# Forty idle products, an earlier key transpose and a reordered first four steps in a gated-recurrence attention plus PReLU network

## The chip, the cores and the metric

The kernel runs on one core of one Trainium2 chip. A core has TensorE (PE, matrix products, with weight loads listed apart as PEld), VectorE (DVE), ScalarE (ACT), GpSimd (POOL) and SyncE (SP, which here only issues DMAs). Each engine works through its own list of instructions in the order in which they stand, and waits on semaphores that other engines and DMAs raise. The metric is the device time of one execution in microseconds (us); lower is better.

## The reference

The first half is a recurrence with a gate, for 4 batches, 8 heads, 768 positions and head size 48. The second half is a two-layer network with a leaky activation over the 3072 tokens, from 384 to 2048 and back to 384. Everything is float32.

```
f = sigmoid(f_logit)
for t in range(768):
    state = f[:, :, t, :, None] * state + outer(k[:, :, t], v[:, :, t])     # 48 x 48 for each head
    y[:, :, t] = q[:, :, t] @ state
x = y.transpose(0, 2, 1, 3).reshape(3072, 384)
h = x @ w_in                                                # 384 -> 2048
g = maximum(h, 0) + alpha * minimum(h, 0)
out = g @ w_out                                             # 2048 -> 384
```

## The kernel before

The sequence is cut into 6 chunks of 128 positions, and the batches into 2 pairs; a *step* is one chunk of one pair, so there are 12 steps, numbered from 0. Steps 0 and 1 are the first chunk of either pair. The work of one step is written as four Python generators, and each `yield` ends a *piece*:

- `prepare` (letter P for the step itself, Q when it belongs to the next step): loads f, q, k and v by DMA, takes the sigmoid on ACT, and forms on DVE the products of gates that scale the queries and keys within a chunk. For chunks after the first, the scaled keys `ks` are turned by one DVE transpose into `kt` (line 424), and 16 small DMAs on SP's queue (line 429) put them in place as `ksn`. In the first chunk PE transposes them instead (`pk`, line 473).
- `carry` (O): PE forms the products across subchunks (`off`, lines 446 and 456) and the chunk's contribution to the state (`pd`, line 486).
- `attend` (S): PE forms the products within blocks of positions (`raw`, line 522, and `qu`, line 537), twice 64 rows each, once for each batch of the pair; DVE copies the wanted parts into `ad` (lines 528 and 543 or 559), ACT moves these into `A` (line 565), PE multiplies by the values and the state (`py`, line 576). ACT copies `py` to `y`, and `y` is put into the network's layout `xT`: by PE in step 0 (`xt`, line 594), by DMAs afterwards.
- `network` (n): 8 groups f0 to f7 of first-layer products (`ph`, line 619, 12 rows of the trace each), ACT's `neg` (line 624) and DVE's `gate` (line 626), DVE sums `S` after each four groups (line 700), then second-layer products (`po` in step 0, line 639; `pa` to `pe` with Strassen-like sums in the others, line 658). The network of one step runs within the attention of the next.

The weights arrive as 64-bit words and are converted in 8 pieces each: a and b are ACT's part of w_in and w_out (two passes over the upper halves, lines 201 and 203), w and v are DVE's part (`lead`, `rest`, `power`, `both`; lines 209, 222, 215, 227 or 229), where POOL issues the DMA that adds the leading part. A call of w forms the lead and power of one piece and finishes the piece before it. W forms sums of w_out's quarters (lines 712 to 720) in memory that the conversion has given back.

The order on PE, DVE and ACT is written out by hand: `first` holds a string of pieces for each of the first four steps, `usual` the one for all others, and the engines' instructions stand in the order in which the pieces are called. Orders on SP and POOL are the tile framework's. PSUM tiles come from two rings: `pair` (2 buffers of two banks, for the attention) and `bank` (4 buffers of one bank, for the network); a product that writes a buffer waits until the tile that had it before has been read.

A float32 product is two weight loads and two matmuls in PE's list, a transpose one of each, and a wait that doesn't fit into an instruction is one instruction more.

Of the kernel before, what the change touches and what calls it, by code (L numbers as in the profile page):

```python
# [8 lines left out]
F32 = mybir.dt.float32  # L9
# [15 lines left out]
NB = DB // 4  # L25
WP = 768
AT_ONCE = 1
RAWS, TOPS, POWERS, LEADS = 4, 3, 1, 4


@with_exitstack
def kernel(
# [30 lines left out]
    nc = tc.nc  # L63
    B, NC, _, HP, _ = qT.shape
# [7 lines left out]
    W = U * HP * C  # L72
# [25 lines left out]
    def bank(name):  # L98
        return psn.tile([128, 512], F32, tag="net", name=name)
# [16 lines left out]
    ones = const.tile([128, NS], F32, tag="ones", name="ones")  # L116
# [17 lines left out]
    for m in range(1, NB):  # L134
        lo = UO[m] + (4 if m == 1 else 0)
        n = NB - m
# [4 lines left out]
    for half in range(2):  # L141
        for m in range(1, NQ):
            n = NQ - m
# [23 lines left out]
    def load_weights(dst, src, name):  # L167
# [16 lines left out]
        words = src.rearrange("p (a n) -> p a n", a=rows_).bitcast(I16)  # L184
        at_once = AT_ONCE if rows_ > 1 else 0
        got = {}
# [66 lines left out]
    def quads(t):  # L253
        return t.rearrange("p (n r) -> p n r", r=4)

    def halves(cc):

        return slice(CH * cc, CH * cc + CH), slice(CH * (1 - cc), CH * (1 - cc) + D)

    def prepare(bp, c, x):  # L260

        i = f"{bp}_{c}"
# [3 lines left out]
        def load(name, src, bufs=2):  # L266
            t = work.tile([128, W], F32, tag=name, name=f"{name}_{i}", bufs=bufs)
            loads.dma_start(out=t.rearrange("p (u x) -> p u x", u=U),
                              in_=src[b0:b0 + U, c].rearrange("u p h t -> p u (h t)"))
            return t  # L270

        f = quads(load("f", fT, 1))
# [3 lines left out]
        for cc in range(NC2):  # L276
            t_, _ = halves(cc)
# [50 lines left out]
        def earlier(m):  # L328

            n = NB - m  # L330
            skip = UO[m - 1] + (8 if m == 2 else 4)
            nc.vector.tensor_tensor(  # L332
                us[:, :, UO[m]:UO[m] + 4 * n].rearrange("p g (i r) -> p g i r", r=4),
                us[:, :, skip:skip + 4 * n].rearrange("p g (i r) -> p g i r", r=4),
                fq[:, :, 1:1 + n].unsqueeze(3).broadcast_to((128, G, n, 4)), ALU.mult)
# [24 lines left out]
        ks = x["ks"] = work.tile([128, GC, 2, DB], F32, tag="ks", name=f"ks_{i}", bufs=1)  # L360
# [38 lines left out]
            earlier(6)  # L399
        nc.vector.tensor_tensor(ks[:, :, 0], kh, f32[:, 1:G:2].broadcast_to((128, GC, DB)), ALU.mult)  # L400
        if c:
            earlier(7)
        else:
            nc.vector.tensor_tensor(q16.rearrange("p g (i r) -> p g i r", r=4), q4[:, :, NQ:NB], g16[:, :, NQ:NB].unsqueeze(3).broadcast_to((128, G, NQ, 4)), ALU.mult)
# [14 lines left out]
                nc.scalar.copy(A[halves(cc)[1], :, par * HP:(par + 1) * HP, CH * cc:CH * (cc + 1)],  # L419
                               q3[rows(par)].rearrange("p (u h c) s t -> p u h c (s t)", h=HP, c=NC2)[:, :, :, cc, 0:CH])  # L420
        if c:

            kt = late["kt"].tile([128, W], F32, tag="kt", name=f"kt_{i}")
            nc.vector.transpose(kt, ks.rearrange("p g s t -> p (g s t)"))
            ksn = x["ksn"] = work.tile([128, U, HP * 128], F32, tag="ksn", name=f"ksn_{i}", bufs=1)
            for a in range(4):
                n = min(32, D - 32 * (a % 2))
                for b in range(NJ):
                    nc.sync.dma_start(
                        out=ksn[32 * b:32 * (b + 1)].rearrange("p u (h x) -> p (u h) x", h=HP)[:, :, 32 * a:32 * a + n],  # L430
                        in_=kt[32 * a:32 * (a + 1)].rearrange("p (g b x) -> p g b x", b=NJ, x=32)[:, :, b, 0:n])
# [257 lines left out]
    late = {}  # L689
# [12 lines left out]
    def halves_of_w_out():  # L702
# [12 lines left out]
        for to, x_, y_, op in ((t3, b22, b12, ALU.subtract), (t2, t3, b11, ALU.add), (t4, t2, b21, ALU.subtract),  # L715
# [3 lines left out]
                nc.vector.tensor_tensor(to[:, p], x_[:, p], y_[:, p], op)  # L719
            yield  # L720

    steps = [(bp, c) for c in range(NC) for bp in range(B // U)]
    first = (
        "P2 a P w P a P a w O P w S a w S Q a O a w S2 Q w S Q S",
        "P a w a P w2 b n2 v O n S b2 v n v n P S b S v n b n S v b v n Q b n b v O v Q n v W Q2 S2 W n Q n W Q W",
        "O W n2 S n2 S Q S n4 O S Q n Q2 n S2 n Q n Q n",
        "n2 S n S n Q n2 O Q O n2 S Q S n S Q n Q S Q n3",
    )
    usual = "S n2 S n2 O2 n Q n2 Q n2 Q S3 n Q S n Q n Q n"
# [6 lines left out]
    def begin(n):  # L736
        if n >= len(steps):
            return [None] * 4
        x = {}
        return [stage(*steps[n], x) for stage in (prepare, carry, attend, network)]  # L740

    with tc.manual_schedule(engines={mybir.EngineType.PE, mybir.EngineType.DVE, mybir.EngineType.Activation}):
        prep, car, att, net = begin(0)
        before = None
        for n in range(len(steps) + 1):
            coming, carried, following, after = begin(n + 1)
            on = pieces | {"P": prep, "O": car, "S": att, "n": before, "Q": coming}
            for key in (first[n] if n < len(first) else usual).split():
                for _ in range(int(key[1:] or 1)):
                    if on[key[0]] is not None:  # L750
                        next(on[key[0]])
            before, prep, car, att, net = net, coming, carried, following, after
# [55 lines left out]
```

## Time and profile before

| | |
|---|---|
| median of 4 runs | 636.97 us (635.4 to 639.11) |
| the profiled execution: its time / its span | 635.78 us / 634.0 us |
| mean granted TensorE clock | 0.994 |
| PE / PEld / DVE / ACT / POOL busy | 588.5 / 524.6 / 505.4 / 249.4 / 67.7 us |
| instructions on PE (matmuls, and as many loads) | 8108 |
| chain that ended last: PE / DVE / issue / ACT / DMA | 84 / 9 / 3 / 2 / 1 % |
| PE busy from 0 to 50 us / 50 to 100 us / 100 to 160 us | 15.7 / 46.0 / 57.9 us |
| PE busy from 300 to 500 us | 199.5 us of 200 |

The profile's times are microseconds from the first instruction's start. A line of a timeline has the start, the length, the engine, the source line, the operation and its tiles with the number of instructions merged, and in brackets the idle time before it with what ended it. "issue" as the cause of a wait means that the profile shows nothing that the engine waited for. PE's ends are modelled and its instructions overlap, so the length of a group is read from the start of one group to the start of the next. The granted clock is the share of full TensorE speed.

### The profile page before, as it was taken

How to read it: one execution, taken by the hardware profiler on the slowest of the kernel's cores; microseconds unless marked ns; L12 is line 12 of the kernel's file. 1: busy time of each engine (PE TensorE's matmuls, PEld its weight loads, DVE VectorE, ACT ScalarE, POOL GpSimd, SP SyncE). 2: the span in 40 equal slices, each digit the busy share in tenths (PEclk: the TensorE clock that was granted, in tenths of full speed). 3: DMA queues.
4: the chain of work that ended last, by engine and by line, in shares of the span. 5: the costliest groups of instructions: out<-in, count | busy, mean ns of one | idle time of the engine just before them, and what ended most of it. 6: DMA issues, size and time to landing. Idle time of an engine off the chain costs nothing.

```text
span 634.0 us, 18857 instructions
## 1 busy us (share of the span) xinstructions
PE 588.5 (93%) x8108; PEld 524.6 (83%) x8108; DVE 505.4 (80%) x1028; ACT 249.4 (39%) x466; POOL 67.7 (11%) x114
## 2 busy tenths in 40 slices
PE   0448799899999999999999999999999999999997
PEld 0447676789889889889889889889889889889997
DVE  5879969999799788888888888888888888762251
ACT  5667682531254053253253253253253253223110
POOL 9132222001001001001001001001001000000000
PEclk9999999989999999999999999999999999999999
DMA  7978987223223313223223222223223211201000
GB/s 243 298 208 217 284 254 163 50 70 78 50 77 85 63 58 84 64 56 84 56 64 84 46 75 85 52 68 84 47 73 79 55 38 26 38 17 26 26 1 25
DMA packets 73122, 56.30 MB, mean 89 GB/s; under 512 B 47408, under 2 KB 64944, under 8 KB 73040
## 3 DMA queue, kind: packets, MB, share of 16 engines
q0 software_dynamic: 10112, 27.53, 16.3%
q1 hardware_dynamic: 57536, 25.37, 15.8%
q10 hardware_dynamic: 5392, 2.21, 1.7%
q8 instruction: 64, 1.05, 0.7%
q14 instruction: 18, 0.15, 0.1%
HBM read 36.21 MB, written 4.72 MB: 65 GB/s over the span
## 4 chain that ended last, share of the span: by engine, by line
PE 84%; DVE 9%; issue 3%; ACT 2%; DMA 1%; DVEq 0%; SPq 0%; ACTq 0%
PE ph L619 38%; PE pc L658 9%; PE pa L658 9%; PE pe L658 5%; PE pd L658 5%; PE pb L658 5%; PE py L576 3%; PE raw L522 3%; PE qu L537 3%; PE pd L486 3%; DVE ad L528 1%; DVE ad L543 1%; PE off L446 1%; DVE t L719 1%; DVE gate L626 1%
## 5 line engine op out<-in xcount | busy, mean ns | idle before, releaser
L619 PE MATMUL ph<-xT,w_in_sb 128*128 128x256 f32 x1152 | 261.0, 385 | 4.0 <-issue 4.0
L619 PEld LDWEIGHTS ph<-xT,w_in_sb 128*128 128x128 f32 x1152 | 218.4, 192 | 36.9 <-issue 6.3
L624 ACT ACTIVATE neg<-ph 128x512 f32<-128x512 f32 x96 | 57.0, 596 | 199.8 <-PE ph L619 154.5
L626 DVE SCALAR_TENSOR_TENSOR gate<-neg,om,ph 128x256 f32<-128x256 f32 x192 | 82.1, 476 | 46.2 <-ACT neg L624 46.0
L658 PE MATMUL pa<-w_out_sb,gate 128*128 128x192 f32 x352 | 62.1, 329 | 0.0
L658 PE MATMUL pc<-t,S 128*128 128x192 f32 x352 | 61.7, 329 | 0.0
L658 PEld LDWEIGHTS pa<-w_out_sb,gate 128*128 128x128 f32 x352 | 57.8, 190 | 1.9 <-DVE gate L626 1.3
L658 PEld LDWEIGHTS pc<-t,S 128*128 128x128 f32 x352 | 57.3, 190 | 0.6
L528 DVE COPY_PREDICATED ad<-mraw,raw 128x256 f32<-128x256 int32 (+1 forms) x96 | 42.3, 440 | 7.6 <-PE raw L522 5.1
L543 DVE COPY_PREDICATED ad<-mquad,qu 128x224 f32<-128x224 int32 (+6 forms) x140 | 42.0, 300 | 6.2
L565 ACT COPY A<-ad 32x256 f32<-32x256 f32 x96 | 38.5, 401 | 1.4
L419 ACT COPY A<-q 48x512 f32<-48x512 f32 x44 | 27.1, 617 | 30.1 <-DVE q L370 29.7
L332 DVE TENSOR_TENSOR us<-us,fs 128x768 f32<-128x768 f32 (+5 forms) x60 | 37.0, 617 | 0.0
L289 DVE TENSOR_TENSOR qd<-qd,f 128x768 f32<-128x768 f32 (+2 forms) x36 | 27.2, 755 | 6.3 <-ACT qd L284 6.3
L576 PEld LDWEIGHTS py<-A,vs 128*64 128x64 f32 x768 | 25.5, 145 | 7.2 <-ACT A L565 4.3
L576 PE MATMUL py<-A,vs 128*64 128x64 f32 x768 | 27.5, 232 | 3.9 <-ACT A L565 3.9
L676 ACT COPY o<-pa 128x192 f32<-128x192 f32 x11 | 3.5, 317 | 69.7 <-PE pa L658 58.5
L700 DVE TENSOR_TENSOR S<-gate 128x512 f32<-128x512 f32 x44 | 30.3, 688 | 0.8
L658 PE MATMUL pe<-w_out_sb,S 128*128 128x192 f32 x176 | 30.5, 327 | 0.4 <-ACT o L676 0.4
L658 PE MATMUL pb<-t,gate 128*128 128x192 f32 x176 | 30.4, 326 | 0.0
L658 PE MATMUL pd<-w_out_sb,S 128*128 128x192 f32 x176 | 30.4, 326 | 0.0
L522 PEld LDWEIGHTS raw<-qd,k 48*32 48x32 f32 x1536 | 18.5, 109 | 14.1 <-issue 13.1
(109 smaller groups left out, 742.0 us busy)
## 6 DMA issues: line engine op xcount, KB each, us to landing
w_out_raw<-in_w_out SPq DMA_DIRECT2D x8, 767.8 KB, 6.5
w_in_raw<-in_w_in SPq DMA_DIRECT2D x8, 767.2 KB, 6.9
f<-in_fT POOLq DMA_DIRECT2D x11, 512.0 KB, 4.5
q<-in_qT POOLq DMA_DIRECT2D x11, 512.0 KB, 4.1
k<-in_kT POOLq DMA_DIRECT2D x11, 512.0 KB, 5.0
out<-o SPq DMA_DIRECT2D x24, 192.0 KB, 2.1
vs<-in_v POOLq DMA_DIRECT2D x22, 192.0 KB, 4.8
w_out_sb<-w_out_lead POOLq DMA_DIRECT2D x8, 384.0 KB, 5.5
```

Source lines behind the costliest of these rows:

```text
L289: nc.vector.tensor_tensor(qdv[d], qdv[d - 1][:, :, :, 1:5 - d], f[:, :, 1:5 - d].rearrange("p (g i) r -> p g i r", i=NB), ALU.mult)
L332: nc.vector.tensor_tensor(us[:, :, UO[m]:UO[m] + 4 * n].rearrange("p g (i r) -> p g i r", r=4), us[:, :, skip:skip + 4 * n].rearrange("p g ...
L522: nc.tensor.matmul(raw[DB * j:DB * (j + 1), par, hp * C:hp * C + QW], lhsT=k[r_, g * DB:(g + 1) * DB], rhs=qd[r_, g], start=True, stop=True)
L528: nc.vector.copy_predicated(adu[:, :, :, d:4], mraw[:, d, :, d:4].bitcast(I32).unsqueeze(1).broadcast_to((128, H, NB, n)), rv[:, :, QO[d]: ...
L543: nc.vector.copy_predicated(ad[:, u, :, :, 4 * m:DB], mquad[:, lo:lo + n].bitcast(I32).unsqueeze(1).unsqueeze(1).broadcast_to((128, 2, HP, ...
L565: nc.scalar.copy(A[s_, u, :, s_], ad[s_, u].rearrange("p r h t -> p (r h) t"))
L576: nc.tensor.matmul(py[64 * par:64 * par + 64, u, o:o + CH], lhsT=vs[bp][:, cc, u, hd * D:hd * D + 64], rhs=A[:, u, par * HP + hp, CH * cc: ...
L619: nc.tensor.matmul(ph[:, j * T:(j + 1) * T], lhsT=w_in_sb[:, kt, m * 128:(m + 1) * 128], rhs=xT[:, kt], start=(kt == 0 and j == 0), stop=( ...
L624: nc.scalar.activation(neg, phv, AF.Relu, scale=-1.0)
L626: nc.vector.scalar_tensor_tensor(gate[:, m % NH, m // NH], neg[:, j], om[:, m:m + 1], phv[:, j], ALU.mult, ALU.add)
L658: nc.tensor.matmul(to[:, 0:DH], lhsT=of(f), rhs=by(f), start=(f == 0 and not more), stop=(f == NH - 1), skip_group_check=True)
L700: nc.vector.tensor_tensor(to, x_, y_, op)
```

## The change

Forty products of 32 x 8 over the constant tile `ones` are put at the head of PE's list; nothing reads their bank. The transpose `kt` moves from the last piece of `prepare` into the piece before it, directly behind the `ks` that it reads; its DMAs stay in the last piece. The four strings of `first` are replaced. `usual` stays.

```diff
+IDLE = 40
 ...
         nc.vector.tensor_tensor(ks[:, :, 0], kh, f32[:, 1:G:2].broadcast_to((128, GC, DB)), ALU.mult)
         if c:
+            kt = x["kt"] = late["kt"].tile([128, W], F32, tag="kt", name=f"kt_{i}")
+            nc.vector.transpose(kt, ks.rearrange("p g s t -> p (g s t)"))
             earlier(7)
 ...
         if c:
-
-            kt = late["kt"].tile([128, W], F32, tag="kt", name=f"kt_{i}")
-            nc.vector.transpose(kt, ks.rearrange("p g s t -> p (g s t)"))
+            kt = x["kt"]
             ksn = x["ksn"] = work.tile([128, U, HP * 128], F32, tag="ksn", name=f"ksn_{i}", bufs=1)
 ...
+    idle = bank("idle")
+
     first = (
-        "P2 a P w P a P a w O P w S a w S Q a O a w S2 Q w S Q S",
-        "P a w a P w2 b n2 v O n S b2 v n v n P S b S v n b n S v b v n Q b n b v O v Q n v W Q2 S2 W n Q n W Q W",
-        "O W n2 S n2 S Q S n4 O S Q n Q2 n S2 n Q n Q n",
+        "P2 a w P2 a P a w O P w S a w S Q a O S a w S Q S Q w S",
+        "P a w a P w2 b n2 O v n b S b v n v n P n S b S v b n S v b v n Q b n O b v Q n v2 W Q2 S2 n Q W n Q W Q W",
+        "O W n2 S n3 S2 n Q n2 O S Q n Q2 n S2 n2 Q n Q",
         "n2 S n S n Q n2 O Q O n2 S Q S n S Q n Q S Q n3",
     )
 ...
     with tc.manual_schedule(engines={mybir.EngineType.PE, mybir.EngineType.DVE, mybir.EngineType.Activation}):
+        for _ in range(IDLE):
+            nc.tensor.matmul(idle[0:32, 0:8], lhsT=ones[:, 0:32], rhs=ones[:, 0:8], start=True, stop=True)
         prep, car, att, net = begin(0)
```

In the lists of the engines this comes to the following. PE: 160 instructions more at the head (two loads and two matmuls for each product); in step 1 the network's group f5 moves ahead of the second `raw` (12 rows), and in step 2 the group f4. DVE: in step 0 the first lead and power stand ahead of line 323; the w that stood before step 1's line 323 stands behind line 355; in step 1 gate f5 moves ahead of the second line 528, the two scans (lines 319 and 321) ahead of a piece of w_out, and the first sums of w_out (line 719) behind line 414; in step 2 gates f4 and f5 move forward with their groups; in all steps from the third on the transpose stands 7 to 12 instructions sooner. ACT: step 0's sixth pass over w_in goes between the two halves of line 565, and some `neg` and conversion passes change places in steps 1 and 2. SP: the first ksn DMAs go ahead of a store of `out`. POOL: two of the loads of v and one of f go ahead of one DMA of the conversion.

## The prediction

> **What bounds the kernel now.** I read the page's slices first, then the windows, the chain of waits, and the PE, DVE and ACT timelines up to 165 us.
>
> From the page (busy tenths in 40 slices; the DMA queue of PE's instructions):
>
> ```profile
> PE   0448799899999999999999999999999999999997
> DVE  5879969999799788888888888888888888762251
> ...
> q8 instruction: 64, 1.05, 0.7%
> ```
>
> From the windows (length, PE busy and instructions, PEld, DVE, ACT, POOL, clock, DMA):
>
> ```profile
> 300.00:400.00 100.00, 99.79 (x1342) 90.91 (x1341) 86.95 (x182) 36.89 (x73) 6.76 (x10) 1.00 0.26 65
> ```
>
> After about 165 us PE has no gap worth naming, so its work there is fixed. The end can move only by time that PE loses before that. From PE's timeline:
>
> ```profile
> 18.49 1.08 PE L446 MATMUL off<-q,kh 48*32 48x32 f32 x64 [18.49 <-DVE q L370]
> 20.12 1.44 PE L456 MATMUL off<-us 48*32 48x16 f32 x128 [0.55 <-DVE us L404]
> 21.49 1.97 PE L473 MATMUL pk<-ident,ks 128*128 128x128 f32 x8
> 23.39 0.75 PE L522 MATMUL raw<-qd,k 48*32 48x80 f32 x22
> 26.76 0.96 PE L522 MATMUL raw<-qd,k 48*32 48x80 f32 x38 [2.62 <-issue]
> ...
> 33.01 0.91 PE L522 MATMUL raw<-qd,k 48*32 48x80 f32 x38 [2.31 <-issue]
> ...
> 39.00 1.20 PE L486 MATMUL pd<-vs,ksn 64*48 64x48 f32 x44 [2.17 <-issue]
> ...
> 76.95 9.48 PE L619 MATMUL ph<-xT,w_in_sb 128*128 128x256 f32 x36 [3.97 <-issue]
> ...
> 126.17 1.07 PE L537 MATMUL qu<-us,k 48*32 48x112 f32 x64 [1.52 <-DVE ad L543]
> ```
>
> Four stops have no releaser. Between the first two lie 42+64+21 = 127 matmuls, between the next two 43+64+20 = 127, with as many loads and two waits: 256 instructions. q8 carries 64 packets of 1.05 MB / 64 = 16 KB, which is 256 of PE's instructions each, and the trace has its packets at 23.7, 30.8, 36.6 and 74.6 us, one near each stop. So PE runs out of instructions. The block after next is asked for when PE enters a block, and in this stage (DMA share 0.8 to 1.0) arrives 5.5 to 6.6 us later: 20.1 to 26.76, 26.76 to 33.01, 33.01 to 39.00, 71.48 to 76.95. A block of small products lasts 2 to 4 us. Later blocks last longer, and packets start about 1 us behind the boundary: no stops.
>
> From ACT's timeline, and from DVE's:
>
> ```profile
> 11.99 0.99 ACT L203 ACTIVATE w_in_neg<-w_in_raw,bias 128x768 int16<-128x768 uint16 x1
> ```
>
> ```profile
> 11.70 1.26 DVE L323 TENSOR_TENSOR us<-us,f 128x1024 f32<-128x1024 f32 x1
> ...
> 14.75 0.55 DVE L209 TENSOR_TENSOR w_in_lead<-w_in_pos,w_in_neg 128x768 bf16<-128x768 bf16 x1
> ...
> 48.41 1.23 DVE L323 TENSOR_TENSOR us<-us,f 128x1024 f32<-128x1024 f32 x1 [2.98 <-ACT us L316]
> ```
>
> Up to 18.5 us DVE sets the pace. From 40.2 us it is ACT: vs, a pass over w_in, eight A copies, four us copies, and y at 48.52. From 88 to 162 us DVE runs without a break; PE waits for it at 123 and 125 us.
>
> **The change, part by part.**
>
> *Lead and power ahead of line 323 (step 0).* They need ACT's neg, which ends at 11.99+0.99 = 12.98; DVE is free at 11.79. Line 323 starts at 12.98+0.05+0.86 (the pair's 14.84 to 15.70) = 13.9 instead of 11.8; the 0.86 no longer stands before line 376. Net +1.25: the first off at 19.75, the second (line 456) at 21.4.
>
> *The idle products.* They wait only for POOL's `ones` (2.1 us) and end long before 18 us even at 0.12 us a row, so their 80 rows cost nothing; the cover is DVE's first chain, and without it they would cost up to 10 us. They shift every block boundary by 160 instructions = 80 rows. The stops then fall on row 79 of line 456, rows 6 and 5 of the two qu, and row 4 of py. The block for the first is asked for 31 instructions behind the first off, which carries only a wait of its own. Does PE's sequencer run that far past a waiting product? One row says yes: the packet of 53.04 us belongs to a boundary on the eighth load of ph, executed at 55.5 us, and lies behind a product whose input (xT, ACT) ended at 52.19; 0.85 us would be the shortest lag of the busy stage, where 1.9 to 4.0 is usual. I take yes: the first block is there by about 12 us. Then, with about 6 us per block: line 456 ends 22.8, pk 24.7, raw 26.4; block asked for at 21.9, there at 28.0; qu to 29.1, raw to 30.75, five rows of qu; next block 34.0; qu to 35.1, pd 35.1 to 37.0 (1.92 for its two parts) instead of 40.20. The next block, at 40.0, is no later than ACT's A copies. **-3.2 at y** (45.3). Bounds: all three stops gone, 1.25-7.1 = -5.9; the sequencer held, first block at 26.0, pd to 41.1: +0.85.
>
> A rule speaks against this. The Trainium skill, "Runtime: NRT & Kernel Launch", section "Instruction fetch mechanics", says that crossing a 16 KiB boundary is mostly hidden; by it the shift is worth nothing and this part +1.25. The four stops of 2.2 to 4.0 us decide for the trace.
>
> *Clock.* pk's 8 transposes take 472 ns each at 21.5 us and 272 at 61.9: PE is slow through the first attention, though the profile lists 1.00. It is listed at 0.50 from 76.5 to 79.9, 3.5 us into the stop. The idle products end some 10 us before the first off, so I give them no gain in speed (bounds: 0, and the 0.9 + 0.3 + 1.0 us by which pk, off and pd exceed their later rows).
>
> The skill's "TensorE: Matmul & The Clock Gate", Part 1, has full speed lost after one idle window of about 3.4 us; by it the gain is zero too.
>
> *Step 1.* The w moved behind line 355 leaves DVE's idle 2.98 and stands in its busy part: 1.76. Line 404 ends at 45.3+11.24+1.73 = 58.3 where PE has done off at 56.6: PE waits 1.6. The block boundary now lies on row 94 of line 456, asked for as off starts (55.8), there at 61 to 62.4: 2.4 more. The next one is on row 8 of qu: 0 to 1.6, take 0.8. With f5 ahead of the second raw, the boundary there has 36 ph rows (8.07) as cover, and the stop of 3.97 goes; with it the half clock (36 rows in 9.33 instead of 8.07: 1.26), of which I put 0.95 back at 56 to 62 us. Sum +0.5, bounds -2 and +2.5. PE reaches po 2.7 earlier. DVE: -3.2+1.76; its idle 2.64+1.72+0.81 at 79 to 88 goes; new idle before line 528, f5 and f7 of 3.8 and 0.7 of slow clock: **-2.1**.
>
> *Step 2.* f4 (2.7 us) ahead of the second raw covers PE's 0.26+1.52, and the half clock of 127.7 to 131.1 (28 rows in 7.93 instead of 6.2) goes: PE 6.2 earlier at line 658's pc. But pc reads S, whose last sum ended at 143.84 where pc began at 145.57, in DVE's unbroken stretch. DVE moves by -2.1, so pc by -2.1-1.73 = **-3.8**. The moved sums of w_out and scans are the same DVE work in another order: 0.
>
> *Transpose sooner, SP's and POOL's order.* In the later steps kt (1.16) passes lines 680 to 682. These free the bank of f0: ready at 305.34, used at 306.94; still 0.44 to spare. ksn's DMAs come about 2.5 us sooner; pd's first products are 0.23 apart in every step, whatever the DMAs do, so that gains only the 0.07 gaps. The store between ksn DMAs waits up to 1 us, and 12 DMAs behind it; they still end 2 us sooner than before. Loads of v and f ahead of one conversion DMA (2 us of POOL's queue): that piece lands about 60 us, used after 66. Shifted boundaries in later steps: one block, near 170 us, of 2.5 us. Together 0, bounds -0.5 and +1.5.
>
> Sum: 635.78-3.8 = 632.0 for an execution like the profiled one, which lies 1.2 under the median; against 636.97 it is **633.2**.
>
> **Rivals.** (1) The sequencer is held by off's wait. For: the other blocks were all asked for as PE reached them. Against: the packet of 53.04. Then +0.85 at y, and DVE's gain is used up: 637.6, slower if blocks take 6.6 rather than 6 us each.
> (2) More stops go: blocks asked for earlier meet a quieter DMA system (5 us each): -5.9 at y and less in step 1: 629.5 to 630.
> (3) Slower: the transpose eats the bank's slack. From 0.44 us of further delay on, f0 waits in each of 8 steps; at 1.16-0.44+0.3 = 1 us each, +8-3.8: 641. Against: DVE's own work before line 680 is unchanged.
>
> **How the numbers follow.** Main case 0.58 (own range 630.5 to 636), rival 1 0.20, rival 2 0.14, rival 3 0.08. About 0.5% (3.2 us) tells a change from none: faster is under 633.8. Main gives 0.36 faster and 0.22 same; rival 1 0.02, 0.13 and 0.05 slower; rival 2 0.14 faster; rival 3 0.08 slower. Range 629.5 to 638.5.
>
> **What would show it.** Right: the first off at 19.7; no stop in line 456 of step 0, stops in both qu near 26 to 28 and 31 to 34; y near 45.3; a stop of 3 to 5 us in line 456 of step 1; none behind the second qu there; clock 1.00 at 127 us; pc following S at once near 141; PE 99.8% busy after. Wrong: a first stop in line 456 of step 0 (rival 1), ph waiting for line 681 in late steps (rival 3).

## The result: no difference that can be measured, and the profile after

The changed kernel takes 637.61 us (median of 45 executions, 632.85 to 642.56), the kernel before 638.37 us (71 executions, 632.05 to 640.75). The ratio is 0.9991, with a 95% interval of 0.9978 to 1.0004: 0.6 us less, between 1.4 us less and 0.3 us more. Forecast were 3.8 us less.

The four times that the prediction had of the kernel before were low: their median of 636.97 is 1.4 us under that of 71 executions, and the execution that was profiled, 635.78, is 2.6 us under it. The profiled execution of the changed kernel, 633.21 us (span 631.4), is 4.4 us under its own median. So the two profiles, set side by side, show a gain of 2.6 us; the medians of all executions differ by 0.8. Single executions of either kernel lie further apart than the whole forecast.

From the changed kernel's page: the slices of PE, DVE and the granted clock, and the queue of PE's instructions.

```profile
span 631.4 us, 19021 instructions
...
PE   2458989999999999999999999999999999999997
...
DVE  5889899999799698888888888888888888762251
...
PEclk9958999999999999999999999999999999999999
...
q8 instruction: 65, 1.06, 0.7%
```

From its windows (length, PE busy and instructions, PEld, DVE, ACT, POOL, clock, DMA share, GB/s):

```profile
0.00:50.00 50.00, 22.58 (x671) 19.53 (x672) 36.67 (x70) 31.64 (x52) 23.36 (x56) 0.83 0.85 250
...
300.00:400.00 100.00, 99.82 (x1456) 90.51 (x1455) 86.83 (x183) 38.20 (x74) 6.76 (x10) 1.00 0.28 66
```

The late steps look as before, PE without a gap. 65 packets of instructions instead of 64: 160 instructions more. From PE's timeline:

```profile
2.16 4.44 PE L747 MATMUL idle<-ones 128*32 128x8 f32 x80 [2.16 <-POOL ones L119]
19.66 1.08 PE L447 MATMUL off<-q,kh 48*32 48x32 f32 x64 [13.07 <-DVE q L371]
21.30 0.98 PE L457 MATMUL off<-us 48*32 48x16 f32 x79 [0.55 <-DVE us L407]
25.28 0.71 PE L457 MATMUL off<-us 48*32 48x16 f32 x49 [3.01 <-issue]
25.92 1.97 PE L474 MATMUL pk<-ident,ks 128*128 128x128 f32 x8
...
30.01 0.77 PE L538 MATMUL qu<-us,k 48*32 48x52 f32 x58 [0.57 <-issue]
...
34.59 1.01 PE L538 MATMUL qu<-us,k 48*32 48x52 f32 x59 [1.84 <-issue]
35.94 1.53 PE L487 MATMUL pd<-vs,ksn 64*48 64x48 f32 x64 [0.34 <-PE qu L538]
...
47.07 4.26 PE L595 MATMUL xt<-y,dense 128*128 128x256 f32 x12 [1.70 <-ACT y L586]
...
58.93 1.25 PE L457 MATMUL off<-us 48*32 48x16 f32 x128 [1.74 <-DVE us L407]
...
76.24 5.45 PE L620 MATMUL ph<-xT,w_in_sb 128*128 128x256 f32 x24
...
137.24 0.59 PE L659 MATMUL pa<-w_out_sb,gate 128*128 128x192 f32 x2 [1.24 <-DVE gate L627]
...
141.05 2.76 PE L659 MATMUL pc<-t,S 128*128 128x192 f32 x16
```

The 80 idle rows are over at 6.6 us. The first off is at 19.66. Then come stops without a releaser, each at the start of an instruction block: row 79 of the second off, row 6 of the first qu, row 5 of the second. The packet of instructions for the first of these stops starts at 22.8 us, and the profile has none of PE's queue, q8, ahead of that. From the DMA view of the changed kernel, 22.8 to 23 us:

```profile
q8 instruction: 1, 0.02, 39.6%
```

xt is at 47.07 where it was at 49.73. The stop of 3.97 us behind step 1's second qu is gone, and pc begins at 141.05 where it began at 145.57.

**How to read a gain in this kernel.** DVE's timelines give one line for each kernel that carries the rest: the last idle time ahead of its unbroken stretch. Of the changed kernel:

```profile
84.89 0.56 DVE L210 TENSOR_TENSOR w_out_lead<-w_out_pos,w_out_neg 128x768 bf16<-128x768 bf16 x1 [0.81 <-ACT w_out_neg L204]
```

Of the kernel before:

```profile
87.98 0.56 DVE L209 TENSOR_TENSOR w_out_lead<-w_out_pos,w_out_neg 128x768 bf16<-128x768 bf16 x1 [0.81 <-ACT w_out_neg L203]
```

From there to the last product there are 543.1 and 542.6 us. Over all 18 profiles of kernels with the full work (these two and 16 below) it is 541.9 to 544.3 us, but for two in which DVE waits once more at 94 us. And from the end of step 0's pd to xt it is 9.5 to 9.6 us in all of them, whatever the order of pieces. So an execution is: the end of pd in step 0, plus 9.6, plus xt to DVE's arrival at that line, plus about 543. Only the first and the third of these terms vary by much: 35.3 to 41.4 and 36.1 to 42.8 us.

### The profile page after: what moved, and what is told of

It reads as the page before. It is cut to its first block, busy times and chain, and to the rows that moved or that the text cites. A ratio compares the mean times of both kernels' runs of the same rounds, so it can differ in the third digit from the quotient of the medians.

```text
span 631.4 us, 19021 instructions
## 1 busy us (share of the span) xinstructions
PE 593.2 (94%) x8188; PEld 528.1 (84%) x8188; DVE 506.6 (80%) x1028; ACT 249.4 (39%) x466; POOL 66.6 (11%) x114
## 4 chain that ended last, share of the span: by engine, by line
PE 71%; DVE 17%; issue 6%; DMA 2%; POOL 2%; ACT 1%; ACTq 0%; DVEq 0%; POOLq 0%
PE ph L620 31%; PE pc L659 8%; PE pa L659 8%; PE pe L659 5%; PE pd L659 4%; PE pb L659 4%; PE py L577 3%; PE qu L538 2%; PE raw L523 2%; PE pd L487 2%; DVE gate L627 2%; DVE ad L529 2%; DVE qd L290 2%; DVE ad L544 1%; DVE S L701 1%
## 5 line engine op out<-in xcount | busy, mean ns | idle before, releaser
L538 PE MATMUL qu<-us,k 48*32 48x112 f32 (+1 forms) x1536 | 26.7, 256 | 3.5 <-issue 2.4
```

The costliest lines, as they stand in the source:

```text
L538: nc.tensor.matmul(qu[DB * j:DB * (j + 1), par, hp * QS + 4:hp * QS + QL], lhsT=k4[r_, g * DB:(g + 1) * DB], rhs=us[r_, g, 4:QL], start=Tr ...
```

## The experiments

All times are set against the kernel before on the same chip (11 to 35 executions of it); 0.1% is 0.64 us. Differences of means, where given, carry their standard error.

### The three parts, alone and together

The change has three parts: idle products (I), the sooner transpose (T), the four strings (S). Their edits:

```diff
I  +        for _ in range(IDLE):
   +            nc.tensor.matmul(idle[0:32, 0:8], lhsT=ones[:, 0:32], rhs=ones[:, 0:8], start=True, stop=True)
T  +            kt = x["kt"] = late["kt"].tile([128, W], F32, tag="kt", name=f"kt_{i}")
   +            nc.vector.transpose(kt, ks.rearrange("p g s t -> p (g s t)"))
                earlier(7)
S  -        "P2 a P w P a P a w O P w S a w S Q a O a w S2 Q w S Q S",
   +        "P2 a w P2 a P a w O P w S a w S Q a O S a w S Q S Q w S",   (and the other three)
```

I alone: 

> The kernel before with the 80 idle products and nothing else. Two readings of the missing gain. The fetch reading: PE's first block after the first off is asked for only when that off runs, and then comes 4.6 to 6.6 us later, execution by execution; the two profiles at hand are two draws of it. By it the first off stays at 18.5, a stop of 3 to 5 us falls on row 79 of the second off, two shorter ones into the two qu; y is 2 to 4 us earlier than before if a fetch takes 4.6 to 5.4 us as in the profile after, 1 us earlier if it takes 6; the stop of 3.97 us at 73 us is gone; the ratio is 0.994 to 0.998. The reading that the idle products gain nothing in the middle execution: ratio 0.999 to 1.001, and whatever is gained by 165 us is lost later, because the blocks are shifted in the later steps too (the profile after lost 1.3 us between 159 us and the end).

S and T, without I: 

> The changed kernel without the idle products. The fetch reading: the first off at 19.7, the old four stops of 2 to 3 us about 1.2 later than before, y 1.2 us later; step 1 loses no stop at 73 us if f5 stands ahead of the second raw; step 2 gains 1.8 us in ad; sum 0 to +1.5 us, ratio 1.000 to 1.002. The reading in which the strings are worth nothing or cost more: ratio 1.003 or above, and then the idle products are a gain that the strings take away.

T alone: 

> The kernel before with the keys transposed sooner and nothing else. My prediction gave it 0 in the later steps. If it is the cause of the 1.3 us that the profile after lost between 159 us and its end: +1 to +1.5 us, ratio 1.002, with small PE gaps at L446 to L537 of the later steps. If it costs nothing: ratio 0.999 to 1.001, and the profile keeps its distance from the profile before from 165 us on within 0.3 us.

All three again: 

> The changed kernel once more, for a second profile and for times beside the parts on the same chip. The fetch reading: again the first off at 19.7 and the first stop on row 79 of the second off, but with fetches that last anything from 4.6 to 6.6 us, so that y lies between 45 and 49; ratio 0.998 to 1.000. The reading that all executions gain 2.6 us, and the equal medians are chance: ratio 0.995 to 0.997.

I and S: 

> The changed kernel with the transpose at its old place: idle products and strings only. On the chip so far, against before: idle products alone 0.9946, strings with transpose 0.9964, transpose alone 1.0016, all three 0.9991 and 0.9994. The reading of a common cap: idle products and strings take away the same waits of DVE ahead of its unbroken stretch (88 to 162 us before), so together they bring no more than the larger of them, and the transpose takes 1 to 2 us back in the later steps: ratio 0.994 to 0.9965. The reading of a clash: the two harm each other in step 1 or 2 whatever the transpose does: ratio 0.998 to 1.000.

S alone: 

> The kernel before with the four new strings alone. Common cap: strings with transpose (0.9964) less the transpose's 1.0016: 0.993 to 0.996. Clash: the same, since there is nothing to clash with. If the ratio is 0.996 to 0.998, the transpose cost nothing beside the strings.

I and T: 

> The kernel before with idle products and the sooner transpose, old strings. Common cap: the two act in different places and add up: 0.9946 times 1.0016 = 0.996, between 0.994 and 0.998. Clash of idle products and transpose (the shifted instruction blocks meet the moved transpose in the later steps): 0.999 or above, the value of the whole change.

| parts | ratio to before | 95% interval | difference of means, us |
|---|---|---|---|
| I | 0.9946 | 0.9918 to 0.9975 | -3.1 (0.9) |
| T | 1.0016 | 0.9996 to 1.0037 | +1.5 (0.5) |
| S | 0.9929; again 0.9962 | 0.9900 to 0.9957; 0.9935 to 0.9988 | -4.2 (0.8); -2.1 (0.9) |
| I T | 0.9965 | 0.9940 to 0.9990 | -1.9 (0.8) |
| S T | 0.9964 | 0.9939 to 0.9990 | -2.0 (0.7) |
| I S | 0.9975 | 0.9949 to 1.0000 | -1.4 (0.7) |
| I S T | 0.9991; again 0.9994 | 0.9978 to 1.0004; 0.9972 to 1.0016 | -0.5 (0.4); -0.3 (0.6) |

Two things follow. The transpose costs where it is added: 1.5 us alone, 1.2 beside I, 0.9 beside I and S, and beside S 2.2 or 0.1, by which run of S is taken; hardly one of them is certain by itself. And I and S each bring 2 to 4 us alone, but 1.4 together, between what the common cap and the clash had expected. The ratios of I alone and T alone lie where the fetch reading and the loss in the later steps had them; S with T is better than either reading allowed.

### Where the transpose costs

Only steps 2 and 3 take the transpose sooner (there `c == 1`), the others as before:

```diff
-        if c:
+        if c == 1:
             kt = x["kt"] = late["kt"].tile([128, W], F32, tag="kt", name=f"kt_{i}")
             nc.vector.transpose(kt, ks.rearrange("p g s t -> p (g s t)"))
```

> The changed kernel with the transpose sooner only in steps 2 and 3, and at its old place in steps 4 to 11. If the loss of the transpose lies in the later steps (0.1 us in each, at the products of f0 behind qu, which wait for line 681): the profile keeps its distance to before from 165 us on, and the time is 0.7 to 1 us under that of the changed kernel, ratio 0.997 to 0.9985. If it lies in steps 2 and 3: as the changed kernel, 0.999 to 1.000.

Measured: 0.9955 (0.9933 to 0.9977), 2.0 us under the changed kernel; more than expected, and in the direction of the late steps. I and S with the transpose at its old place everywhere have 0.9975 on the same chip, so none of the cost is left. From DVE's arrival to the last product it is 542.8 us here, and 543.6 on average (542.7 to 544.3) in the six profiles with the whole T, against 542.7 (541.9 to 543.1) in the nine without T; the two profiles in which DVE waits once more are left aside. The transpose alone shows the place. DVE of that kernel in a late step:

```profile
400.20 1.25 DVE L403 STREAM_TRANSPOSE kt<-ks 128x1024 f32<-128x1024 f32 x1
...
403.99 0.35 DVE L681 TENSOR_TENSOR o<-Csum,pb 128x192 f32<-128x192 f32 x1
```

Its PE, at the end of step 2 and in the same late step:

```profile
162.66 5.45 PE L619 MATMUL ph<-xT,w_in_sb 128*128 128x256 f32 x24 [1.54 <-DVE Csum L680]
...
403.73 1.16 PE L537 MATMUL qu<-us,k 48*32 48x112 f32 x62
404.81 0.48 PE L619 MATMUL ph<-xT,w_in_sb 128*128 128x256 f32 x1
```

DVE of the kernel before in that late step:

```profile
400.39 0.35 DVE L681 TENSOR_TENSOR o<-Csum,pb 128x192 f32<-128x192 f32 x1
```

And its PE:

```profile
401.37 1.04 PE L537 MATMUL qu<-us,k 48*32 48x112 f32 x62
402.37 2.83 PE L619 MATMUL ph<-xT,w_in_sb 128*128 128x256 f32 x12
```

Lines 680 to 682 read the banks that the next network groups write. Before, line 681 ended at 400.74 and f0 began at 402.37, 1.63 us later. With the transpose ahead of it, it ends at 404.34 and f0 begins at 404.81, still 0.47 later, but 1.08 behind qu's start instead of 1.00. Between 175 and 600 us the stretches from qu to the network's next group grow by 0.6 to 0.7 us in sum in the four profiles of T, S T and I S T (two); without T they grow by 0.3 us at most. The rows show no idle time of PE there, so that f0 is late because of its bank is argued, not shown. Where f0 comes early it is shown: at 162.66 it waits 1.54 us for line 680. I T has this wait too (1.60 us); the kernels with the new strings don't, so for them the late stretches are what is left.

### The phase of PE's instruction blocks

One block is 256 of PE's instructions, which are 64 idle products. n of them move every later boundary by 2n rows. The first four kernels are the new strings with the old transpose, and differ only in this number:

```diff
-IDLE = 40
+IDLE = 0 / 64 / 4 / 56
```

0: 

> The kernel before with the new strings alone, once more, as the base of three kernels that differ from it only in the number of idle products. Expected 0.993 of before, 0.991 to 0.996. Its instruction blocks end on row 22 of the first raw, row 21 of the second and row 20 of pd in step 0, and in step 1 on row 26 of the first raw and row 51 of the second qu: profile with a stop of 2 to 3 us there, near 75 to 80 us.

64: 

> New strings and 64 idle products, which are 256 instructions: exactly one block more, so every boundary in the attention lies on the row where it lies without idle products. The reading that idle products act only by shifting the blocks: as the strings alone, within 0.2%, profile with the stop on row 51 of step 1's second qu. The reading that the products themselves do the harm (or the good), by the array, its clock, or the bank that they take: as with 40 of them, 0.9975.

4: 

> New strings and 4 idle products, 8 rows of shift. The block reading, with a fetch of about 5.5 us: in step 0 boundaries on rows 14, 13 and 12 of raw, raw and pd, as good as without; in step 1 on row 18 of raw (5.9 us behind the boundary before it), row 17 of the ph group behind the first qu (5.0 us) and row 43 of the second qu (5.4 us): every block has nearly its fetch time, and the stop of 2 to 3 us at the second qu goes; 2 to 2.5 us less than the strings alone, ratio 0.989 to 0.991. If the phase is nothing: as the strings alone.

56: 

> New strings and 56 idle products, a phase that should be bad: in step 1 a boundary on row 62 of the second off comes 3.2 us behind the one before, and one on row 3 of the ph group behind the second qu 2.1 us behind the one before it: stops of 2.3 and 3.4 us by a fetch of 5.5 us, where the strings alone have one of 2.5. Step 0 as without idle products (rows 38, 37 and 36). Block reading: 2.5 to 3.5 us more than the strings alone, ratio 0.997 to 0.999. If the phase is nothing: as the strings alone.

56 again, on another chip: 

> New strings, transpose at its old place, 56 idle products, once more, to see whether 0.9908 (6 executions) stands. If the phase of the instruction blocks is what counts: 0.989 to 0.993. If it was the draw: 0.995 to 0.997, as the strings alone and with 64.

The whole changed kernel with 56: 

> The changed kernel with 56 idle products in place of 40, and nothing else. If the change is lost to the phase at 40 and to the transpose: 0.992 to 0.995, the phase of 56 less 0.2% for the transpose. If the phase is nothing: 0.998 to 1.000, as the changed kernel.

The kernel before with 56: 

> The kernel before with 56 idle products and nothing else: old strings, old transpose. If the phase of the blocks is what 56 brings, the strings being worth little beside it: 0.989 to 0.994. If 56 is good only with the new strings, whose group f5 stands between its two boundaries of step 1: as with 40 idle products alone, 0.994 to 0.997.

The changed kernel with 40 at the head and 16 more ahead of xt in step 0, so that the blocks of 40 hold in step 0 and those of 56 from step 1 on:

```diff
         if not (bp or c):
+            more = bank("more")
+            for _ in range(16):
+                nc.tensor.matmul(more[0:32, 0:8], lhsT=ones[:, 0:32], rhs=ones[:, 0:8], start=True, stop=True)
```

> The changed kernel with its 40 idle products at the head and 16 more directly ahead of xt in step 0, where PE waits 1.7 us for y: step 0 keeps the blocks of 40, and from step 1 on they lie as with 56. Between 0.9992 (40) and 0.9908 (56) lie 5.4 us. By the profiles (4 with 40 and the new strings, 3 with 56) 2.0 us of it lie ahead of pd's end in step 0 and about 1 us in step 1, at row 94 of the second off. If step 0 makes most of it: 0.996 to 0.999. If step 1 and later make most of it: 0.991 to 0.994.

| strings, transpose | idle products | ratio to before | 95% interval |
|---|---|---|---|
| new, old | 0 | 0.9962 | 0.9935 to 0.9988 |
| new, old | 64 | 0.9967 | 0.9945 to 0.9988 |
| new, old | 4 | 0.9923 | 0.9896 to 0.9951 |
| new, old | 56 | 0.9908; again 0.9903 | 0.9878 to 0.9938; 0.9869 to 0.9938 |
| new, sooner | 40 | 0.9991 | 0.9978 to 1.0004 |
| new, sooner | 56 | 0.9908 | 0.9876 to 0.9939 |
| new, sooner | 40, and 16 later | 0.9967 | 0.9943 to 0.9991 |
| old, old | 56 | 0.9926 | 0.9899 to 0.9954 |

0 and 64 differ by 0.05%, and their profiles stop on the same rows: 22, 21 and 20 of raw, raw and pd, and step 1's second qu (2.33 and 2.61 us). So as far as these runs show, the products do nothing but move the boundaries. The phase decides: sixteen products more, 56 in place of 40, turn the change from nothing into 0.9%. With those 16 put behind step 0's attention, 0.24 of the 0.83 points come back. By the means, 3.3 us (1.3) of what lies between 40 and 56 would so belong to step 0 and 1.7 us (0.8) to what follows; which part is the larger these runs can't say.

My forecasts of single phases were poor. 4 came out at 0.9923 against 0.9962 for 0, in the expected direction but short of the 0.989 to 0.991, with intervals that overlap; and its stops in step 1 (1.54 and 1.03 us) are in sum hardly less than those with 0 (0.46 and 2.33). 56 was to be a bad phase, by its boundaries in step 1 and a fetch of 5.5 us everywhere; it is the best that was tried, with no stop at row 62 of the second off and 1.77 us at ph. With 56 the kernels with the new strings are 0.2% ahead of the one with the old, which these runs can't tell from none.

What the phase does in step 0 can be looked at in seven profiles with 40 and eleven with other numbers. Two of them, on the same piece of PE's timeline. New strings with 40 (the run with the transpose in two steps, an execution with late blocks):

```profile
21.42 0.98 PE L462 MATMUL off<-us 48*32 48x16 f32 x79 [0.55 <-DVE us L408]
26.94 0.71 PE L462 MATMUL off<-us 48*32 48x16 f32 x49 [4.54 <-issue]
...
34.14 1.01 PE L543 MATMUL qu<-us,k 48*32 48x52 f32 x58 [3.14 <-issue]
...
37.82 1.02 PE L543 MATMUL qu<-us,k 48*32 48x52 f32 x59 [1.09 <-issue]
39.81 1.53 PE L492 MATMUL pd<-vs,ksn 64*48 64x48 f32 x64 [0.97 <-PE qu L543]
```

New strings with 56 (the first run with it, an execution with early blocks):

```profile
21.49 1.44 PE L457 MATMUL off<-us 48*32 48x16 f32 x128 [0.55 <-DVE us L405]
...
30.08 0.64 PE L523 MATMUL raw<-qd,k 48*32 48x80 f32 x22 [0.35 <-issue]
...
33.30 1.95 PE L487 MATMUL pd<-vs,ksn 64*48 64x48 f32 x64 [1.62 <-issue]
```

In either case PE needs three blocks on its way to the end of pd. With 40 the third begins on row 5 of the second qu, and 2.9 to 3.8 us of work stand behind it. With 56 it begins on row 36 of pd: 0.9 us (no stop there in this execution; the 1.62 us at pd's first row are another wait, 1.24 in the kernel before). In the kernel before it is row 20: 1.2 us. The blocks themselves come when they come: the first resume lies between 25.3 and 28.6 us in all 18, whether the block was asked for at 18.7 (old strings, 40) or at 21.5 to 21.9 (new strings, other numbers). The third is 1.5 us earlier on average with 40 (36.1 against 37.6 us), but has 2.4 us more of work behind it.

That 40 loses its time in step 0 is not shown by this. The pd of step 0 ends at 39.6 us on average with 40, at 39.4 in the seven profiles with 0, 4 or 64, and at 37.4 in the four with 56, with about 1 us of standard error on each difference: 56 looks good there rather than 40 bad. And the old strings have step 0's boundaries on the same rows with 40 and with 56, but lie much closer together: 0.9946 and 0.9926. In step 1, 40 puts a boundary on row 94 of line 456, asked for when off starts. One profile, of I and S, paid for it in full:

```profile
60.96 0.97 PE L457 MATMUL off<-us 48*32 48x16 f32 x94 [0.49 <-DVE us L405]
65.67 0.45 PE L457 MATMUL off<-us 48*32 48x16 f32 x34 [3.74 <-issue]
```

The five others with that boundary have 0 to 0.8 us there; the mean of the six is 0.9. So the profiles show 39.6 - 37.4 = 2.2 us (1.1) and 0.9 us of the 5 that lie between 40 and 56. The rest a handful of executions doesn't resolve. The seven profiles with 40, and no other, also have PE wait 0.9 to 2.0 us at 89 to 96 us for a piece of w_out; since DVE carries the rest from there, it doesn't show in the time from DVE's arrival to the last product.

### Where the fetch time comes from

w_in's pieces 2 to 7 take their words from piece 1:

```diff
-            raw = stage.tile([128, WP, 4], I16, tag="raw", name=f"{name}_raw{n}", bufs=RAWS)
-            nc.sync.dma_start(...)
+            if n < 2 or rows_ == 1:
+                raw = stage.tile([128, WP, 4], I16, tag="raw", name=f"{name}_raw{n}", bufs=RAWS)
+                nc.sync.dma_start(...)
+                first_raw.append(raw)
+            else:
+                raw = first_raw[1]
```

In the kernel before: 

> The kernel before without the loads of six of w_in's eight pieces: pieces 2 to 7 are converted from the words of piece 1, so the first layer's weights are wrong; all other work stays. It takes 4.6 MB of bulk loads out of the DMA system between 10 and 45 us. If PE's instruction blocks arrive late because they stand behind bulk loads: fetches from the entry of a block to the resume fall from 3.9 to 8.0 us (10 profiles) to 2 to 3.5 us in step 0, the four stops of 2.2 to 2.6 us there shrink to under 1 us each, y comes 4 us or more earlier, and the times of single executions differ less. If the fetch has a latency of its own: stops as before, 5.5 us apart or more.

In the changed kernel: 

> The same omission in the changed kernel. With cheap fetches in step 0 the idle products have nothing to move there, the first lead and power ahead of line 323 stay at +1.25 us, the transpose stays at +1.4, and step 1's stop at 73 us is still there to be saved: within 0.3% of the light kernel before on either side. If the change's parts are worth what my prediction gave them in step 1 and 2: 2 to 3 us faster than the light kernel before.

Measured: 0.9882 (0.9834 to 0.9930) and 0.9908 (0.9880 to 0.9937) of the kernel before; four executions each, 627.5 to 635.4 and 632.0 to 633.8 us. PE of the light kernel before:

```profile
23.52 0.75 PE L527 MATMUL raw<-qd,k 48*32 48x80 f32 x22
25.39 0.95 PE L527 MATMUL raw<-qd,k 48*32 48x80 f32 x38 [1.12 <-issue]
...
28.58 1.77 PE L527 MATMUL raw<-qd,k 48*32 48x80 f32 x59 [1.34 <-DVE ad L533]
...
33.14 1.53 PE L491 MATMUL pd<-vs,ksn 64*48 64x48 f32 x64 [1.83 <-issue]
```

Of the stops at block boundaries in step 0 only the first is left, with 1.12 us (pd's 1.83 is at its first row, not at row 20); xt came 5.5 us earlier, at 44.26. From the entry of a block to the next resume it is 4.9 us there, and 4.9, 4.7 and 3.4 us in the changed light kernel, where the full kernels have 3.4 to 7.9. I had expected 2 to 3.5 us. Each of these values occurs in full kernels too, so the sums alone show little. But a fetch can be split where its packet starts. From the entry of the block to the packet it is 1.0 to 5.4 us in the 54 fetches of the 18 full profiles up to pd (mean 3.0), and 1.1 to 2.4 us (mean 1.7) in the six of the light ones; from the packet to the resume it is 2.2 to 3.1 us in both. So what is drawn anew is the time until the packet starts, and as far as two profiles show, bulk loads make it longer; the 2.2 to 3.1 us behind it stay without them. That the executions would differ less did not show in the kernel before. The two light kernels lie 0.26 points apart, inside the 0.3% that was expected, and four executions each can't tell that from nothing. In the profiles xt is 2.8 us later in the changed one (47.02 against 44.26), of which 1.5 is the first off at 20.13 instead of 18.62.

## Why the prediction was wrong

**The baseline was one draw.** Every duration was taken from one execution, as it must be, and that execution was placed 1.2 us under a median of four. It lay 2.6 us under the real one. More to the point: the prediction took three fetches of about 6 us as properties of the stage. They are draws from 3.4 to 7.9 us, and the sum of three moves the end of step 0 by 6 us: its pd ends between 35.3 and 41.4 us in 18 profiles. By two of its times the prediction looks nearly right on the changed kernel's profile: y begins at 45.85 against 45.3, and pc at 141.05 against "near 141". That is luck. Two of its signs failed there: line 456 of step 0 has a stop (3.01 us), and line 456 of step 1 has none within. And the profile had fetches of 5.4, 4.7 and 4.6 us; the four other profiles with the new strings and 40 have xt at 47.6 to 51.0 instead of 47.1.

Point by point:

- *Lead and power ahead of line 323, +1.25*: the first off came 1.2 later, at 19.66 against 19.75. But on average it isn't paid: the first resume is at 26.5 us in the five profiles with the old order as in the thirteen with the new.
- *Idle products, -3.2 at y*: this step failed. "I take yes: the first block is there by about 12 us" was wrong. PE did not enter the block behind the first off while that off waited; the packets are at 22.8 us and later, and the first stop is on row 79 of line 456, which the prediction had named as the sign of its first rival. The stops fall on the rows that it gave for the boundaries (79, 6 and 5). Its one row for the yes, a packet 0.85 us behind its wait "where 1.9 to 4.0 is usual", was no proof: step 0's packets start 1.0 to 5.4 us behind the entry of a block. In place of the -3.2 the profiles show no gain: xt is at 49.1 us on average in the five with the new strings and 40, at 49.7 and 48.1 in the two with the old strings and none. What idle products bring beside the old strings (0.9946) comes behind xt, where the stop of 3.97 us goes: from xt to DVE's arrival it is 36.6 and 36.9 us with 40, 38.2 and 40.7 without. Rival 1 had the mechanism. That its 637.6 is also the measured median is luck: it stood for 0.6 us more than a baseline that was 1.4 us too low.
- *The fetch rule of the skill.* The Trainium skill, "Runtime: NRT & Kernel Launch", section "Instruction fetch mechanics", has a crossing of 16 KiB mostly hidden. The stops of up to 4.8 us at boundaries, and 5 us between two numbers of idle products, say that here it isn't. To count the stops against the page was right; what the prediction made of them was not.
- *Clock, nothing from the idle products*: right. pk's eight transposes take 1.97 us in the changed kernel as before.
- *Step 1, +0.5*: the stop of 3.97 us and the half clock behind it went, as said; the new stop in line 456, put at 2.4, is 0 in this profile, 0.4 in the second and 3.7 in that of I and S. The prediction had DVE lose 1.1 us from y to its arrival (-3.2 to -2.1). From xt to the arrival it is 37.8 and 38.2 us in the two profiles, against 38.2 before: no loss, and no gain either.
- *Step 2, PE -6.2 but pc bound by S*: right in kind. PE was 6.5 us ahead at pd, pa waited 1.24 us for gate, and pc followed at -4.5. What DVE had gained ahead of 88 us is all that was left. In this profile it arrived 3.1 us sooner; the five with the new strings and 40 have 84.9 to 91.9 us, the two with the old strings and no idle products 88.0 and 88.8, so on average there is next to nothing.
- *Transpose sooner, 0*: a mis-sized term. It costs about 0.9 to 1.5 us. The slack of f0 was put at 0.44 us after the move, and 0.47 is there; still f0 comes 0.1 us later in five or six of the sixteen late stretches, which the sum had at nothing, and with the old strings it waits 1.5 us once, at the end of step 2, where it comes early. The third rival forecast f0 late in each step, by 1 us; what was seen is a tenth of that.

What stays open: why the new strings are worth 0.4 to 0.7% without idle products, 0.2% with 56 (in the noise), and cost 0.3% with 40 (0.9975 against 0.9946 for the idle products alone). A part can be read from the time between xt and DVE's arrival. With the old strings, idle products (40 or 56) bring it from 38.2 and 40.7 to 36.1 to 36.9 us. With the new ones it is 38.0 to 40.6 with 0, 4 or 64, and 37.8 to 38.3 in seven of the eight profiles with 40 or 56: less is left for them to gain. The eighth has the stop of 3.74 us on row 94 of line 456. That boundary is in the kernels with the old strings and 40 too, and the long stop was seen once, with the new strings; that it happens often there is argued, not shown.

## What to carry to other kernels

Where a stage is bound by events that are drawn anew in each execution, two profiles can't be subtracted: here they said 2.6 us and the medians 0.8. Look for the point from which everything is fixed (here DVE's arrival at 83 to 92 us), and judge an edit by its mean there. A stage of many small products can be paced by the delivery of its instructions, as step 0 is here; adding a few dummy products to move the block boundaries is a knob of its own, to be scanned, since the value can't be worked out from one profile: 56 in place of 40 made this change 0.9908, and with the transpose back in its place 0.9903 to 0.9908 of the kernel before, faster than either kernel.

## What the runs showed of the hardware

- In step 0 of all 18 profiles the packet with PE's next block of instructions started after PE had entered the block before it: in the changed kernel PE entered one at 19.9 us, the packet started at 22.8, and PE could go on at 25.3. It is 3.4 to 7.9 us from the entry of a block to the first row of the next; 256 instructions of small products last 2 to 4 us. (The prediction says "the block after next"; its own rows, 26.76 to 33.01, are one block apart.)
- The second fetch of step 0 has two kinds of values: 3.7 to 4.8 us in five profiles, where pd ends at 35.3 to 38.0, and 5.1 to 7.6 us in the thirteen others, where it ends at 38.3 to 41.4. What makes the difference was not found.
- The granted clock is listed as 1.00 where there is no record yet. The records begin at 52.6 us in the profile before and at 29.5 us in the one after, so the window from 0 to 50 us has 1.00 before and 0.83 after, while pk takes 1.97 us in both.
